# An mLSTM cell followed by a GELU block: the last weight conversion in the front's order, and two unread products

## The chip, the cores and the metric

The kernel runs on one core of a Trainium2 chip. The metric is the device time of one execution in microseconds. A core has a matrix engine (TensorE, PE in the profile; its weight loads are shown as PEld), a vector engine (VectorE, DVE), a scalar engine (ScalarE, ACT), a general engine (GpSimd, POOL) and a queue that issues the transfers (SyncE, SP). Each works through its own list of instructions and waits for the others by semaphores.

## The reference

Two blocks are computed one after the other. The first is a recurrent cell with 4 batches, 8 heads, 768 steps and head size 40, in float32:

```python
for t in range(S):
    m_new = np.maximum(f_gate[:, :, t] + m, i_gate[:, :, t])
    f_stab = np.exp(f_gate[:, :, t] + m - m_new)
    i_stab = np.exp(i_gate[:, :, t] - m_new)
    m = m_new
    C = f_stab[..., None, None] * C + i_stab[..., None, None] * np.einsum('bhd,bhe->bhde', vt, kt)
    n = f_stab[..., None] * n + i_stab[..., None] * kt
    h_tilde = np.einsum('bhde,bhe->bhd', C, qt)
    nq = np.einsum('bhd,bhd->bh', n, qt)[:, :, None]
    y[:, :, t] = sigmoid(o_gate) * h_tilde / np.maximum(np.abs(nq), 1.0)
```

The second takes y as x, of 3072 tokens by 320, and computes `gelu(x @ w_in) @ w_out` with w_in of 320 x 2048 and w_out of 2048 x 320. The weights arrive as float64 and are taken apart on the chip, as two 32-bit words each.

## The kernel before

The 768 steps are cut into 6 chunks ("cells") of 128, and each cell works on its 4 batches one after the other. Inside a cell the recurrence is written as matrix products: scores of keys and queries, weighed by decays, times the values, plus what the state of the cells before brings. The y of a cell (512 tokens) is transposed into x and goes through the up projection, GELU and down projection.

There is no scheduler: the order is written by hand. Each engine's list follows from the order in which the Python code emits the instructions. For the first stretch, "the front" (the first two cells, the conversion of all weights, and the first cell's up and down projection), the order is the string `FRONT`; each word is a letter for a step and, for most, a number of a batch. `play` runs it word by word. The words that matter here:

- `E`, `N`: `second_gates` and `later_gates`, the sums and running maxima of the gates of cell 1 and of cells 2 to 5 on VectorE, a store of the maxima, turns of `a` on TensorE (L216) and the two exponentials on ScalarE (L239, L240).
- `D`, `Q`: turns of the decays `ew` and `gg` into `ewT` and `gT` (TensorE L216, copies on VectorE L217). `d`, `q`: `decays_last`, a product with `last` (L249, tile `pd`) and its copy into `dec` (L251).
- `k2`: `warm(2)`, two products into a tile `cold` that nothing reads (L198). Each f32 product shows as two matmul records.
- `w`, `m`, `g`, `t`, `s`, `c`, `v`, `y`, `x`: steps of cell 0 for one batch (weights, mask, gate, turn, scores, carry, values, finish, turn of y); in capitals those of cell 1. `R`: `split_x`, which takes x_hi away from the transposed y (`px`) and writes x_lo and x_all on VectorE (L587, L588).
- `K`: `conv_one`, the first half of the conversion of the next piece of weights: VectorE L326, L331 and L333, with two ScalarE instructions, L328 and L329, between them. `J`: `conv_two`, the second half: VectorE L340 and L343. Pieces 0 to 9 are w_in, pieces 10 to 25 are the 16 rows of w_out. `J` also fetches the piece four further on, if there is one.
- `F`: one of the 16 rows of the first cell's down projection, four products with one row of w_out (L782, eight records). After the last row ScalarE copies the four results out (L787).
- `Z`: `split_weight`, which makes the high part of a w_in piece on ScalarE (L625) and its low part on VectorE (L627).

After the front, the loop over the cells calls `up` (L729 and L740: three products, of high, low and mixed parts, of each pair of w_in columns; the mixed weights are joined on VectorE, L633; GELU on ScalarE, L744) and then the down projection of the cell by seven products of sums (L805), between which the steps of the next cell are put by the string `DOWN`.

Tiles come from pools with a fixed number of buffers for a tag. Of weight here: `ps_tr` with two banks for all transposes (`pg`, `pd`, `pt`, `px`), `ps_h` with two banks for `cold`, `pf` and `ph`. A new tile waits until the one that had its buffer has been read.

Of the kernel before, what the change touches and what calls it, by code (L numbers as in the profile page):

```python
# [25 lines left out]


FRONT = """
    I2 O0 g0 L0 P0 L1 E k1 t0 P1 P2 k7 w0 N w1 O1 K L2 Q s0 O3 w2 q D d k2 P3 t1 w3 c0 L3 J v0 t2 K K y0 s1 I7 v1 I8
    O2 J g1 L4 I5 c1 K I1 I2 y1 s2 x0 t3 B4 O4 B5 g2 J x1 s3 v2 c2 L5 y2 H T0 x2 G0 v3 g3 c3 K y3 M1 J L6 J A x3 M0 K  # L30
    W0 O7 K A O6 O5 J M2 W1 S0 C0 K J J T1 U U K L7 V0 K T2 J J A G2 K G1 Y0 W2 S1 K M3 C1 A J S2 J K W3 K V1 C2 Y1
    T3 J J U U S3 V2 K K J G3 J Y2 C3 X0 K V3 J K F J F K K B8 F J K F F J K F F F R0 X1 J J K F J F K X2 F J K F J
    Y3 Z F R1 F K J B9 B10 F X3 R2 Z R3 F"""
DOWN = """
    M0 Z M1 W0 F L3 F W1 Z Z F S0 Z S1 K2 C0 M2 Z C1 G0 G1 G2 G3 V0 Z V1 W2 Z M3 F Q2 K3 Q3 Y0 D3 F F W3 F Z S2 S3
    C2 C3 V2 V3 F N F Y1 X0 R0 Y2 F F Y3 X1 R1 F X2 R2 F X3 R3 F"""
# [890 lines left out]
```

## Time and profile before

| what | us |
|---|---|
| three runs, middle one | 487.4 |
| the three runs | 485.79, 487.40, 490.38 |
| the profiled execution | 485.45 |
| its span, first to last instruction | 483.7 |
| TensorE busy | 474.4 |
| VectorE busy | 344.9 |
| ScalarE busy | 222.4 |
| granted TensorE clock, share of full | 1.00 |

The span is what the trace covers; the profiled execution's own time is 1.75 us longer. In the lines below, L followed by a number is a line of the kernel; `po<-w_out,g` is written from `w_out` and `g`; x with a number counts instructions; a bracket gives the time that the engine sat idle before the instruction and what ended that. Instructions on one engine overlap a little[...]. In the chain of waits the times are those of the chain alone, without overlap.

### The profile page before, as it was taken

The numbers are of one execution on the slowest core, as the hardware profiler recorded it, in microseconds if no ns is written. First come the engines' busy times: TensorE is split into PE (matmuls) and PEld (weight loads), VectorE is DVE, ScalarE is ACT, GpSimd is POOL, SyncE is SP. The second block draws the span as 40 slices with busy tenths as digits, with TensorE's granted clock in tenths as the row PEclk, the third lists the DMA queues.
The fourth block names the chain that finished last, engine by engine and source line by source line (L and its number), as shares of the span: only waits on it lengthen the run. The fifth ranks groups of instructions, "written<-read, shape, count | busy, mean of one in ns | idle before, by whom it ended". The sixth has DMA issues, their size and how long they took to land.

```text
span 483.7 us, 10808 instructions
## 1 busy us (share of the span) xinstructions
PE 474.4 (98%) x4224; PEld 415.5 (86%) x4224; DVE 344.9 (71%) x728; ACT 222.4 (46%) x477; POOL 70.2 (15%) x108
## 2 busy tenths in 40 slices
PE   8899999999999999999999999999999999999996
PEld 7687888877677999977999977999977899977996
DVE  7899699898979988747497857498757397724321
ACT  6977999844532942211961212961202861211300
POOL 3001210001000136200144200145000221000000
PEclk9999999999999999999999999999999999999999
DMA  9998965379320355931274922265921250100001
GB/s 176 200 216 185 191 160 138 102 174 224 95 26 4 40 113 75 209 59 21 31 145 67 200 41 25 30 134 94 184 42 22 32 87 3 54 3 0 1 1 54
DMA packets 164434, 44.24 MB, mean 91 GB/s; under 512 B 154176, under 2 KB 157408, under 8 KB 164384
## 3 DMA queue, kind: packets, MB, share of 16 engines
q1 hardware_dynamic: 164384, 43.56, 46.2%
q8 instruction: 33, 0.54, 0.5%
q14 instruction: 17, 0.14, 0.1%
HBM read 39.52 MB, written 4.01 MB: 90 GB/s over the span
## 4 chain that ended last, share of the span: by engine, by line
PE 79%; DVE 13%; ACT 3%; issue 1%; DMA 1%; POOL 1%; SPq 1%; DVEq 0%; POOLq 0%
PE po L805 30%; PE pu L729 21%; PE pu L740 6%; PE pu L674 5%; PE ps L471 5%; PE ph L534 4%; PE pf L495 2%; PE pf L490 2%; DVE w_out L343 1%; PE pu L680 1%; DVE pow L340 1%; PE px L569 1%; PE pt L445 1%; DVE W L474 1%; DMA W<-M_d 1%
## 5 line engine op out<-in xcount | busy, mean ns | idle before, releaser
L805 PE MATMUL po<-w_out,g 128*128 128x160 f32 x640 | 91.2, 300 | 0.0
L744 ACT ACTIVATE g<-pu 128x512 f32<-128x512 f32 x80 | 40.8, 614 | 108.2 <-PE pu L740 108.0
L805 PEld LDWEIGHTS po<-w_out,g 128*128 128x128 f32 x640 | 87.8, 190 | 1.8 <-ACT g L744 1.8
L402 ACT ACTIVATE W<-W,aT 128x128 f32<-128x128 f32 x160 | 48.9, 389 | 2.3 <-POOL W L376 2.2
L805 PE MATMUL po<-w_sums,sums 128*128 128x160 f32 x320 | 47.2, 302 | 0.0
L805 PEld LDWEIGHTS po<-w_sums,sums 128*128 128x128 f32 x320 | 44.2, 190 | 0.4
L579 ACT ACTIVATE x_hi<-px 128x384 fp32r<-128x384 f32 x20 | 9.8, 490 | 71.6 <-PE px L569 71.6
L729 PE MATMUL pu<-x_hi,w_in_hi 128*128 128x512 f32 x160 | 41.4, 401 | 0.0
L474 DVE TENSOR_TENSOR W<-ps,W 128x512 f32<-128x512 f32 x48 | 30.2, 683 | 15.2 <-ACT W L402 10.7
L729 PE MATMUL pu<-x_lo,w_in_lo 128*128 128x512 f32 x160 | 40.6, 396 | 0.0
L661 DVE TENSOR_TENSOR sums<-g 128x512 f32<-128x512 f32 x20 | 13.8, 690 | 33.3 <-ACT g L744 33.3
L376 POOL TENSOR_SCALAR_AFFINE_SELECT W<-W 128x1024 f32<-128x1024 f32 x20 | 23.1, 1162 | 92.7 <-DMA W<-M_d 92.4
L729 PEld LDWEIGHTS pu<-x_hi,w_in_hi 128*128 128x128 f32 x160 | 29.4, 188 | 8.2 <-ACT g L744 1.9
L782 PE MATMUL po<-w_out,g 128*128 128x320 f32 x128 | 35.3, 434 | 1.1 <-DVE w_out L343 1.1
L729 PEld LDWEIGHTS pu<-x_lo,w_in_lo 128*128 128x128 f32 x160 | 30.1, 188 | 7.2
L782 PEld LDWEIGHTS po<-w_out,g 128*128 128x128 f32 x128 | 24.0, 190 | 10.9 <-DVE w_out L343 1.4
L818 DVE TENSOR_TENSOR o_sb<-po,o_sb 128x320 f32<-128x320 f32 (+1 forms) x27 | 12.6, 465 | 28.3 <-PE po L805 24.4
L729 PE MATMUL pu<-x_all,w_in_mid 128*128 128x512 f32 x80 | 31.7, 396 | 0.1
L729 PE MATMUL pu<-x_all,w_mid 128*128 128x512 f32 x80 | 31.7, 396 | 0.0
L414 POOL MEMSET g<- 32x1024 f32 x8 | 7.6, 945 | 157.9 <-ACT W L402 157.7
L633 DVE TENSOR_TENSOR w_in_mid<-w_in_hi,w_in_lo 128x512 fp32r<-128x512 f32 x20 | 13.8, 688 | 21.6 <-PE pu L729 21.6
L674 PE MATMUL pu<-first_x,w_in 128*128 128x256 f32 x128 | 29.1, 382 | 0.1
(169 smaller groups left out, 884.2 us busy)
## 6 DMA issues: line engine op xcount, KB each, us to landing
W<-M_d SPq DMA_DIRECT2D x20, 512.0 KB, 5.7
bits<-in_moe_w_in_dram SPq DMA_DIRECT2D x20, 256.0 KB, 4.2
bits<-in_moe_w_out_dram SPq DMA_DIRECT2D x16, 320.0 KB, 3.5
ob<-in_o_gate_dram SPq DMA_DIRECT2D x24, 160.0 KB, 3.8
out_dram<-o_sb SPq DMA_DIRECT2D x24, 160.0 KB, 1.9
vb<-in_v_dram SPq DMA_DIRECT2D x22, 160.0 KB, 5.2
kb<-in_k_dram SPq DMA_DIRECT2D x22, 160.0 KB, 4.9
blocks<-in_k_dram SPq DMA_DIRECT2D x48, 32.0 KB, 2.2
```

Source lines behind the costliest of these rows:

```text
L376: nc.gpsimd.affine_select(out=t, in_=t, compare_op=OP.is_ge, fill=1.0e30, base=0, pattern=[[0, H], [1, L]], channel_multiplier=-1)
L402: nc.scalar.activation(out=W[n][:, h, :], in_=src, func=AF.Exp, scale=-1.0, bias=aT[:, self.c, r:r + 1])
L471: nc.tensor.matmul(ps[hip][:, p, :], kT[r, p, :], qT[r, p, :], start=True, stop=True)
L474: nc.vector.tensor_tensor(out=w, in0=ps[hip], in1=w, op=OP.mult)
L534: nc.tensor.matmul(ph[r, h, :], Pm[:, h, r], vb[turn_of(n)][:, h, :], start=True, stop=True)
L633: nc.vector.tensor_tensor(out=w_mid[i], in0=w_hi[i], in1=w_lo[i], op=OP.add)
L674: nc.tensor.matmul(banks[-1][e][:, i - i0, :], in_tile(i, x)[:, e, i % 2 * P:(i % 2 + 1) * P], first_x[:, x, t0:t1], start=(x == 0 and i = ...
L729: nc.tensor.matmul(pus[i][e], w[k][:, e, i * P:(i + 1) * P], x[:, k, :], start=(n == 0 and k == 0), stop=False, skip_group_check=True)
L740: nc.tensor.matmul(pu[e], w[r, i // 2, i % 2 * P:(i % 2 + 1) * P], x[r, NX, :], start=False, stop=(n == 2), skip_group_check=True)
L744: nc.scalar.activation(out=g.t[:, HF * e + i, :], in_=pu[e], func=AF.Gelu, scale=4097.0)
L782: nc.tensor.matmul(po[b], g.t[:, f, b * L:(b + 1) * L], w_out[:, f, :], start=(f == 0), stop=(f == NF - 1))
L805: nc.tensor.matmul(bank[at][:, i, :], lhs(j, t), rhs(j), start=(first and i == 0 and j == 0), stop=(i == n - 1 and j == HF - 1), skip_grou ...
```

## The change

Two places in the string `FRONT` are rewritten. Near its beginning one more `k2` is put behind `N`, and the `k2` that stood behind `d` is put ahead of it. At its end, the last `K` goes ahead of the row `F` that follows the finish of batch 3, the last `J` goes between the split of x1 and the next row, and the first `Z` goes behind that row. The list is printed anew, so line breaks in it move as well; words that are not named stay in their order.

```diff
-  ... k7 w0 N w1 O1 K L2 Q s0 O3 w2 q D d k2 P3 t1 ...
+  ... k7 w0 N k2 w1 O1 K L2 Q s0 O3 w2 q D k2 d P3 t1 ...
...
-  ... X2 F J K F J Y3 Z F R1 F K J B9 B10 F X3 R2 Z R3 F
+  ... X2 F J K F J Y3 K F R1 J F Z B9 B10 F X3 R2 Z R3 F
```

The instructions of TensorE are the same but for the two unread products (four records) that are new and the two that trade places with the product of `d`. On VectorE and ScalarE none is added; the conversion of piece 25 (`K`, `J`) comes ahead of the low and high weight of `Z`. The orders of GpSimd and SyncE are the same.

More of the change, by code (lines that the diff above doesn't have):

```diff
@@ L28 @@
 FRONT = """
[L29 to L33, printed above, removed]
+    I2 O0 g0 L0 P0 L1 E k1 t0 P1 P2 k7 w0 N k2 w1 O1 K L2 Q s0 O3 w2 q D k2 d P3 t1 w3 c0 L3 J v0 t2 K K y0 s1 I7 v1
+    I8 O2 J g1 L4 I5 c1 K I1 I2 y1 s2 x0 t3 B4 O4 B5 g2 J x1 s3 v2 c2 L5 y2 H T0 x2 G0 v3 g3 c3 K y3 M1 J L6 J A x3
+    M0 K W0 O7 K A O6 O5 J M2 W1 S0 C0 K J J T1 U U K L7 V0 K T2 J J A G2 K G1 Y0 W2 S1 K M3 C1 A J S2 J K W3 K V1 C2
+    Y1 T3 J J U U S3 V2 K K J G3 J Y2 C3 X0 K V3 J K F J F K K B8 F J K F F J K F F F R0 X1 J J K F J F K X2 F J K F
+    J Y3 K F R1 J F Z B9 B10 F X3 R2 Z R3 F"""
 DOWN = """
```

## The prediction

> **What bounds the kernel now.** I read the share of each engine first, then the chain of work that ended last, then who waited for whom at the two places that the diff touches, then the timeline there. The first view says that TensorE (PE) is the limit over the whole span, and the chain by engine says how much of the end is not TensorE's.
>
> ```profile
> PE 474.4 (98%) x4224; PEld 415.5 (86%) x4224; DVE 344.9 (71%) x728; ACT 222.4 (46%) x477; POOL 70.2 (15%) x108
> PE 79%; DVE 13%; ACT 3%; issue 1%; DMA 1%; POOL 1%; SPq 1%; DVEq 0%; POOLq 0%
> ```
>
> So only what makes TensorE wait, or what feeds the 13% of VectorE (DVE) on the chain, can count. The chain around the end of the front reads (start, us, work):
>
> ```profile
> 122.62 0.93 DVE y_rest L558
> 123.55 0.60 DVE w_in_lo L627
> 124.15 0.47 DVE x_lo L587
> 124.62 0.46 DVE x_all L588
> 125.08 0.24 DVE pow L326
> ...
> 125.35 0.57 ACT pow L328
> ...
> 127.07 0.50 DVE w_out L343
> 127.57 0.04 issue
> 127.62 2.42 PE po L782 x8
> 130.04 11.17 PE pu L729 x48
> ```
>
> The reader is to see that the eight products of the last row of the first down projection begin at 127.62, 0.05 us after VectorE has written the last w_out row. The wait in front of them is in the timeline of TensorE:
>
> ```profile
> 126.20 0.27 PE L569 MATMUL px<-ident,y_rest 128*128 128x128 f32 x1
> 127.62 2.42 PE L782 MATMUL po<-w_out,g 128*128 128x320 f32 x8 [1.14 <-DVE w_out L343]
> ```
>
> That idle time, 1.14 us, is all that TensorE has left at this place. The other place is the gates' turn near 19 us:
>
> ```profile
> 18.26 0.25 PE L216 MATMUL pg<-ident,gg 32*128 32x32 f32 x1
> 18.54 0.19 DVE L217 COPY gT<-pg 128x32 f32<-128x32 f32 x1 [0.17 <-PE pg L216]
> 18.79 0.41 PE L249 MATMUL pd<-gT,last 128*128 128x32 f32 x2 [0.28 <-DVE gT L217]
> 19.04 0.69 PE L198 MATMUL cold<-w_out 128*128 128x128 f32 x4
> 19.24 0.19 DVE L251 COPY dec<-pd 128x32 f32<-128x32 f32 x1 [0.50 <-PE pd L249]
> 19.56 0.60 PE L445 MATMUL pt<-ident,kb 128*128 128x128 f32 x4
> ```
>
> TensorE idles 0.28 us for gT, and VectorE 0.50 us for pd. One unread f32 product is two matmul records, so a k2 is the row "cold x4".
>
> **What the Trainium skill says.** "TensorE: Matmul & The Clock Gate", Part 1, says that TensorE runs at half clock until it has been busy for a window of about 3.4 us. The trace agrees: 12 cold matmuls took 2.75 us from 4.16 (0.23 each), 14 took 1.73 us from 9.22 (0.12 each), and later pt groups of four keep 0.60 us. So unread products have no clock to win at 12 to 20 us in this execution. "PSUM — Partial Sum Buffer", section "Engine vs sequencer instructions", says that VectorE's and ScalarE's queues are strictly first in, first out, and that matmuls complete in order. The records of this trace keep that order, so what is moved on VectorE moves everything behind it.
>
> **The change part by part.**
>
> *Conversion of piece 25 (w_out row 15).* Five VectorE and two ScalarE (ACT) instructions move; none is added or removed. SyncE's and GpSimd's orders are unchanged, and no load follows, for no piece is left to fetch. VectorE's order from the end of y_rest was: low weight, split of x1, first half of the conversion, second half, split of x2. It becomes first half, split of x1, second half, low weight, split of x2. The first slot stays where y_rest leaves it, at 123.47 (start of the low weight in the timeline). Durations from start to start: the first half followed by a split took 1.01 (L326 at 108.83, split at 109.84); a split took 0.94 (124.07 to the next work at 125.00 is 0.93); L340 took 0.52 (110.92 to 111.44) and L343 itself 0.49. So: split at 123.47 + 1.01 = 124.48; L340 at 125.42; L343 at 125.94, done at 126.43; products possible at 126.43 + 0.05 = 126.48. The two ScalarE steps lie beside the split: L328 began 0.35 after L326 and the pair ended 1.51 after it (125.00, 125.35, 126.51), so they end at 124.98, before 125.42. The former wait of 0.47 us for L329 is gone. TensorE is free at 126.20 + 0.27 = 126.47. The start moves from 127.62 to 126.48: **1.14 us less**; I take 1.1. Its ends: 0 if something else holds the products (below), 1.14 at most, since no idle time is left.
>
> What is late next? The low weight 0 starts at 126.34 in place of 123.47, split x2 at 126.94, low weight 1 at 127.87, split x3 at 128.47, ending at 129.40 (129.94 before, so 0.5 earlier). The low products started at 131.73 and would start at 130.6; x_lo is whole at 129.02. The mid products started at 133.60, now 132.5; their weights follow at 130.1 and 130.7. Cover remains in both, 1.6 and 1.8 us. On ScalarE the high weight 0 goes behind L329 and ends at 124.98 + 0.61 = 125.6, and VectorE wants it at 126.34. The transposes of x3 need the PSUM buffer that split x1 frees: 125.08 before, 125.49 now, against 125.98, when TensorE gets there; slack 0.49, cost nothing. The copies of po (ScalarE, four in 2.04 us) find high weight 1 done at 127.5, so they end near 129.5, ahead of the second pair of banks at 134.4.
>
> Does the gain travel? TensorE runs from 130.04 without a break in the chain to 142.14; then g on ScalarE, w_rest_hi, the low weights and sums on VectorE, and TensorE again at 154.10. Each link starts from the one before, so a whole chain shifts. VectorE idles 2.15 us before 141.06, waiting for buffers that these products free, so it has room.
>
> *k2 put ahead of d.* One product pair, 0.52 us (19.04 to 19.56), starts right after the turn of gg, at about 18.35 (18.26 and one spacing of such turns, (0.43 - 0.25) / 3 = 0.06 us, and rounding up). It ends issuing at 18.87, against 18.79, when gT is there. So pd and dec are 0.1 us late, at most 0.25 (if the pair starts at 18.51, after the turn's full record), and TensorE reaches pt 0.2 to 0.45 us sooner. Does being sooner help? VectorE works from dec at 19.24 to 31.44 with no idle time in its records, and TensorE meets it at the ph products at 26.82 (the W product of L474 ends at 26.87) and at px, 31.52, whose ob ends at 31.44. So TensorE would wait there, and VectorE's lateness travels: +0.1, between 0 and +0.25. Behind dec queue vw and the conversion of piece 0; pf at 21.41 needs vw, which ends at 19.84, so that wait is covered. Below nothing: the 0.18 us that VectorE waits at 31.62 could be saved, but px stays tied to ob, so I exclude more than 0.05.
>
> *New k2 behind N.* Four records of 0.13 us follow the turns of a (11.76, four of them, issuing done near 12.0), so they end near 12.52. The mask products pm were waiting for ScalarE's W until 12.62 (0.43 us idle). ScalarE takes that pm only after ew and gg, at 14.91. Cost nothing; if that cover were gone, 0.52. Nothing reads the tile; it takes one more turn of the pool of two.
>
> Sum: -1.1 + 0.1 + 0 = **-1.0 us**. The profiled execution took 485.45 us (span 483.7, 1.75 around it), so like it 484.45. The three runs shown are 485.79, 487.4 and 490.38; with the profiled one the middle of four is (485.79 + 487.4) / 2 = 486.6. Less 1.0 this is 485.6, which I predict; against the median of 487.4 it would be 486.4.
>
> **The rivals.** *The gain is taken back* (chance 0.2). TensorE starts earlier, but a later meeting with VectorE (the mid weights of pair 3, on the chain at 152.76) is set by VectorE's own 0.5 us instead of by TensorE's 1.1, or later than that by loads. For it: VectorE is busy 24.91 of the 29 us from 131 to 160. Against it: the 2.15 us hole. Time: 486.6 - 0.5 + 0.1 = 486.2, or 486.7 with nothing left.
>
> *Both places gain* (0.12). The idle 0.28 us before pd is filled for nothing and TensorE's lead of 0.44 us survives because VectorE catches up. Against it stands the unbroken work of VectorE. Time: 486.6 - 1.14 - 0.4 = 485.1.
>
> *Slower: unread products at the low clock* (0.13). The window's phase differs between executions. If TensorE is still at the rate of 4.16 us, a pair costs 4 x 0.23 = 0.92 us, two 1.84. Placed ahead of pd and pm, both would have to lie wholly on the chain; it decides from the point where they add more than 1.1 us. Then 486.6 + 1.84 - 1.1 = 487.3. For it: runs of one kernel spread over 4.6 us. Against it: pm has cover of over 2 us until 14.91.
>
> That the change does not do what it says is small here: the new order on VectorE and ScalarE is as the list of steps reads. My own case has 0.55.
>
> **How the numbers follow.** The range begins below the second rival on the profiled execution's level (485.45 - 1.54 = 483.9) and reaches over the slow rival on the level of the median (487.4 + 0.74 = 488.1): 483.8 to 488.4. A measurement of this kernel can tell about 1%, 4.9 us, from no change; every case lies far inside that. What remains is the scatter of the runs: faster 0.03, same 0.92, slower 0.05.
>
> **What would show it.** Right: the wait of the last L782 products for w_out under 0.2 us, they start about 1.1 us earlier counted from the first of them, the wait for L329 ahead of the last L340 gone, dec within 0.25 us of its place, and pu's first L729 group followed by the low products without a wait. Wrong: a wait of L569 for px's buffer, of L729 for x_lo or w_in_lo, a longer idle time before dec, or the start of the second cell's first po products (158.99 before) less than 0.6 us earlier.

## The result, and the profile after

Both kernels were run 22 times side by side: 484.19 us after (483.64 to 486.20) against 485.69 us before (484.14 to 490.38), both medians. The ratio is 0.9969, with a 95% interval of 0.9955 to 0.9983: 1.5 us (0.3%) less, and the whole interval lies below 1. The page of the changed kernel shows a span 1.2 us shorter, with four TensorE matmul records more (the new k2) and the same count on the other engines:

```profile
span 482.5 us, 10815 instructions
PE 474.3 (98%) x4228; PEld 415.3 (86%) x4228; DVE 348.3 (72%) x728; ACT 222.1 (46%) x477; POOL 69.8 (14%) x108
```

The chain of waits at the end of the front (start, us, work) now stays on TensorE:

```profile
115.58 10.77 PE po L782 x40
126.35 0.33 PE px L569 x3
126.68 0.04 issue
126.72 2.42 PE po L782 x8
129.14 11.15 PE pu L729 x48
```

In the chain of before, VectorE and ScalarE stood ahead of the last eight products; here the transposes of x3 do, by a narrow margin: w_out ended at 126.66. VectorE's own timeline shows the new order, and no wait for L329 in front of L340:

```profile
123.58 0.23 DVE L558 COPY y_rest<-ob 128x128 f32<-128x128 f32 x1
123.73 0.32 DVE L326 TENSOR_SCALAR pow<-bits 128x320 uint32<-128x320 uint32 x1
...
124.72 0.55 DVE L587 SCALAR_TENSOR_TENSOR x_lo<-px,x_hi 128x384 fp32r<-128x384 f32 x1
...
125.65 0.48 DVE L340 SCALAR_TENSOR_TENSOR pow<-bits,pow 128x320 uint32<-128x320 uint32 x1
126.17 0.49 DVE L343 SCALAR_TENSOR_TENSOR w_out<-sig,pow 128x320 f32<-128x320 f32 x1
126.58 0.69 DVE L627 SCALAR_TENSOR_TENSOR w_in_lo<-w_in_hi,w_in 128x512 fp32r<-128x512 f32 x1
```

At the gates' turn the two lines of VectorE are

```profile
18.61 0.19 DVE L217 COPY gT<-pg 128x32 f32<-128x32 f32 x1 [0.17 <-PE pg L216]
19.40 0.19 DVE L251 COPY dec<-pd 128x32 f32<-128x32 f32 x1 [0.59 <-PE pd L249]
```

From gT to dec it is 0.79 us; before it was 0.70 (18.54 to 19.24). TensorE's timeline has the `k2` ahead of pd:

```profile
18.51 0.71 PE L198 MATMUL cold<-w_out 128*128 128x128 f32 x4
19.05 0.31 PE L249 MATMUL pd<-gT,last 128*128 128x32 f32 x2
```

One execution differs from the next by some tenths of a microsecond before and between these places, so I compare distances inside a profile rather than times of day. "First to last row" is from the first L782 product to the first of the last eight; the mark of the stage after it is the first L805 product; "stage" is from there to the next up projection's first L729; "mask" is from the L805 mark to GpSimd's second mask of cell 2 (L376).

| distance, us | before | after | difference |
|---|---|---|---|
| gT copy to first L782 | 74.38 | 74.51 | +0.13 |
| first to last row of L782 | 34.70 | 33.60 | -1.10 |
| last row to first L805 | 31.30 | 31.28 | -0.02 |
| stage | 44.67 | 44.25 | -0.42 |
| mask | 20.87 | 20.39 | -0.48 |

So the profile's 1.2 us are the end's 1.1 and 0.42 us in a stage that the diff does not touch, less some tenths in which the front and the last cells took longer. That stage, and why the medians show 1.5, needed experiments.

The distance from the first to the last row has a scatter of its own: over all profiles of this study it is 34.68 to 35.01 in the six kernels with the old end and 33.39 to 33.73 in the six with the new one. A sharper measure starts at VectorE's "slot", the first instruction behind the last y_rest. Before, that is

```profile
123.47 0.68 DVE L627 SCALAR_TENSOR_TENSOR w_in_lo<-w_in_hi,w_in 128x512 fp32r<-128x512 f32 x1
```

and the products of the last row start at 127.62, 4.15 us later. After, it is L326 at 123.73, and the products start at 126.72, 2.99 us later. In all six kernels with the old end this path takes 4.14 or 4.15 us, in all six with the new end 2.99 or 3.00. What scatters is the place of the slot, 30.39 to 30.87 us behind the first row, and part of that is GpSimd's mask near 122 us (L376), which stretches one or another of the VectorE instructions ahead of it. In the changed profile it stretches L550 to 0.94 us (0.17 before), with the end and the new k2 it stretches L552 to 1.05 (0.49 before): 0.77 and 0.56 us lost, which is the 0.2 by which their slots differ (30.61 and 30.39).

### The profile page after: what moved, and what is told of

The parts are those of the page before. It is cut to its first block, busy times and chain, and to the rows that moved or that the text cites. A ratio compares the mean times of both kernels' runs of the same rounds, so it can differ in the third digit from the quotient of the medians.

```text
span 482.5 us, 10815 instructions
## 1 busy us (share of the span) xinstructions
PE 474.3 (98%) x4228; PEld 415.3 (86%) x4228; DVE 348.3 (72%) x728; ACT 222.1 (46%) x477; POOL 69.8 (14%) x108
## 4 chain that ended last, share of the span: by engine, by line
PE 89%; DVE 6%; DMA 1%; ACT 1%; issue 1%; SPq 1%; DVEq 0%
PE po L805 32%; PE pu L729 21%; PE po L782 7%; PE pu L740 6%; PE pu L674 5%; PE ps L471 4%; PE ph L534 4%; PE pf L495 3%; PE pf L490 2%; PE px L569 2%; PE pu L680 1%; DMA v<-in_v_dram 1%; ACT g L744 1%; PE pt L445 1%; SPq L135 1%
## 5 line engine op out<-in xcount | busy, mean ns | idle before, releaser
L805 PE MATMUL po<-w_out,g 128*128 128x160 f32 x640 | 91.2, 300 | 0.0
L805 PEld LDWEIGHTS po<-w_out,g 128*128 128x128 f32 x640 | 87.8, 190 | 1.8 <-ACT g L744 1.8
L805 PE MATMUL po<-w_sums,sums 128*128 128x160 f32 x320 | 47.2, 302 | 0.0
L805 PEld LDWEIGHTS po<-w_sums,sums 128*128 128x128 f32 x320 | 44.2, 190 | 0.4
L729 PE MATMUL pu<-x_hi,w_in_hi 128*128 128x512 f32 x160 | 41.4, 400 | 0.0
L729 PE MATMUL pu<-x_lo,w_in_lo 128*128 128x512 f32 x160 | 40.6, 396 | 0.0
L729 PEld LDWEIGHTS pu<-x_hi,w_in_hi 128*128 128x128 f32 x160 | 29.4, 188 | 8.2 <-ACT g L744 1.9
L729 PEld LDWEIGHTS pu<-x_lo,w_in_lo 128*128 128x128 f32 x160 | 30.1, 188 | 7.2
L376 POOL TENSOR_SCALAR_AFFINE_SELECT W<-W 128x1024 f32<-128x1024 f32 x20 | 22.5, 1132 | 91.4 <-DMA W<-M_d 74.5
L782 PE MATMUL po<-w_out,g 128*128 128x320 f32 x128 | 35.3, 434 | 0.0
L782 PEld LDWEIGHTS po<-w_out,g 128*128 128x128 f32 x128 | 24.0, 190 | 9.8 <-DVE w_out L343 0.3
L729 PE MATMUL pu<-x_all,w_in_mid 128*128 128x512 f32 x80 | 31.7, 396 | 0.1
L729 PE MATMUL pu<-x_all,w_mid 128*128 128x512 f32 x80 | 31.7, 396 | 0.0
```

The source lines that it names most:

```text
L376: nc.gpsimd.affine_select(out=t, in_=t, compare_op=OP.is_ge, fill=1.0e30, base=0, pattern=[[0, H], [1, L]], channel_multiplier=-1)
L729: nc.tensor.matmul(pus[i][e], w[k][:, e, i * P:(i + 1) * P], x[:, k, :], start=(n == 0 and k == 0), stop=False, skip_group_check=True)
L782: nc.tensor.matmul(po[b], g.t[:, f, b * L:(b + 1) * L], w_out[:, f, :], start=(f == 0), stop=(f == NF - 1))
L805: nc.tensor.matmul(bank[at][:, i, :], lhs(j, t), rhs(j), start=(first and i == 0 and j == 0), stop=(i == n - 1 and j == HF - 1), skip_grou ...
```

## The experiments

This is what the kernel before, the changed kernel and the twelve experiments gave. The last three columns sort the timed runs by their mean granted TensorE clock; "at full clock" is 0.998 or more. The kernel before was timed beside the experiments in four comparisons, which its row puts together; the median of its runs at full clock is 485.28 to 485.55 in the four, so a difference of 0.2 us between kernels of different comparisons says nothing. Its 22 runs beside the changed kernel have no clock on record and are not in the row.

| kernel | median us, runs | ratio to before, interval | runs at full clock, their median | 0.995 to 0.997 | under 0.995 |
|---|---|---|---|---|---|
| before | 486.31, 217 | | 118, 485.43 | 54 | 45 |
| changed | 484.19, 22 | 0.9969, 0.9955 to 0.9983 | 18, 484.11 | 4 | 0 |
| end only | 484.84, 22 | 0.9959, 0.9937 to 0.9980 | 13, 484.33 | 8 | 1 |
| both k2 only | 485.56, 22 | 0.9976, 0.9956 to 0.9996 | 19, 485.53 | 3 | 0 |
| Z behind only | 485.04, 22 | 0.9981, 0.9956 to 1.0006 | 13, 484.91 | 5 | 4 |
| K split only | 485.98, 22 | 0.9998, 0.9972 to 1.0024 | 10, 485.05 | 7 | 5 |
| eight ahead of d | 488.11, 12 | 1.0023, 0.9994 to 1.0052 | 5, 486.63 | 5 | 2 |
| eight behind N | 485.52, 20 | 0.9961, 0.9940 to 0.9981 | 20, 485.52 | 0 | 0 |
| W first | 489.13, 22 | 1.0049, 1.0025 to 1.0073 | 10, 487.87 | 9 | 3 |
| end, W first | 487.33, 22 | 1.0008, 0.9985 to 1.0032 | 13, 486.96 | 4 | 5 |
| end, new k2 | 484.67, 22 | 0.9972, 0.9952 to 0.9993 | 16, 484.47 | 5 | 1 |
| end, eight behind N | 483.95, 11 | 0.9958, 0.9941 to 0.9976 | 11, 483.95 | 0 | 0 |
| the same again | 484.37, 22 | 0.9962, 0.9947 to 0.9977 | 22, 484.37 | 0 | 0 |
| no k2 | 486.38, 22 | 1.0010, 0.9989 to 1.0031 | 10, 485.50 | 7 | 5 |

### The two halves of the change

End only:

```diff
-  ... Y3 Z F R1 F K J B9 B10 F X3 R2 Z R3 F
+  ... Y3 K F R1 J F Z B9 B10 F X3 R2 Z R3 F
```

> Only the end of the front is changed; the unread products stay as before. Theory A (the order of VectorE ahead of the last w_out row is all of the gain, the two k2 cost a little): the wait of the last L782 products falls from 1.14 to under 0.2 us, dec keeps its place at 19.24, the products of the first down projection begin at 92.9 as before, and the kernel is 1.1 to 1.6 us faster than before, as fast as the changed kernel or 0.1 us faster. Theory B (the unread products bring the gain, or half of it): less than 0.6 us faster.

Both k2 only:

```diff
-  ... k7 w0 N w1 ... q D d k2 P3 ...
+  ... k7 w0 N k2 w1 ... q D k2 d P3 ...
```

> Only the two k2 are changed; the end of the front stays as before. Theory A: pd about 0.1 us later counted from gT, VectorE behind it too, the first L782 product about 0.1 to 0.2 us later, the wait of 1.14 us for w_out unchanged, and the kernel 0 to 0.3 us slower, which the times can hardly tell from none. Theory B: 0.6 us faster or more.

With the end alone the distance from the first to the last row fell from 34.70 to 33.73, and TensorE's timeline shows what is left of the wait:

```profile
127.03 2.42 PE L782 MATMUL po<-w_out,g 128*128 128x320 f32 x8 [0.17 <-DVE w_out L343]
```

At full clock its runs are 485.43 - 484.33 = 1.1 us faster (1.0 against the 485.32 of the kernel before in the same comparison), the size forecast for the end. One expectation missed: the first row began at 93.30 and not near 92.9, 75.00 us behind gT in place of 74.38. With W first and the same front (below) it is 74.36, so this is one execution's scatter. With the two k2 alone the distance stayed at 34.69 and the wait at 1.13; gT to dec grew from 0.70 to 0.78 (18.55 to 19.33), gT to the first row by 0.06, and at full clock the runs are 0.1 us slower (0.2 in the same comparison). So theory A holds for both halves as far as runs at full clock go. Yet the ratio to before is 0.9976, with the whole interval below 1: the last columns of the table say why, and they come back below.

### The end, term by term

Z behind only:

```diff
-  ... Y3 Z F R1 F K J B9 B10 F X3 ...
+  ... Y3 F R1 F K J Z B9 B10 F X3 ...
```

> Of the end only one move: the first Z goes behind the last J; K and J stay together behind the split of x1. Theory A, term by term: the low weight's 0.60 us leaves the path to w_out row 15, the wait for L329 (0.47 us) stays, so the wait of the last L782 products is 1.14 - 0.60 = 0.54 us and the kernel about 0.6 us faster. Rival (the wait of the last products is set by something beside VectorE's list): the wait stays near 1.14 or goes at once.

K split only:

```diff
-  ... Y3 Z F R1 F K J B9 B10 F X3 ...
+  ... Y3 Z K F R1 J F B9 B10 F X3 ...
```

> Of the end only the other move: the conversion's first half ahead of the split of x1 and its second half behind it, with the first Z still ahead of both. Theory A, term by term: VectorE has 0.60 of low weight, 1.01, 0.94, 0.52 and 0.49 us to do from 123.47, so w_out is there at 127.03 and the wait is about 0.6 us; the wait for L329 is gone; the kernel is about 0.5 us faster. With the run in which only Z goes behind, the two gains add up to the whole 1.1. Rival: as there.

The slot on VectorE and the last row on TensorE with only Z behind:

```profile
123.52 0.55 DVE L587 SCALAR_TENSOR_TENSOR x_lo<-px,x_hi 128x384 fp32r<-128x384 f32 x1
127.06 2.42 PE L782 MATMUL po<-w_out,g 128*128 128x320 f32 x8 [0.62 <-DVE w_out L343]
```

and with only K split, where the transposes of x3 (px) are of interest too:

```profile
123.62 0.68 DVE L627 SCALAR_TENSOR_TENSOR w_in_lo<-w_in_hi,w_in 128x512 fp32r<-128x512 f32 x1
126.38 0.41 PE L569 MATMUL px<-ident,ob 128*128 128x128 f32 x2
126.63 0.27 PE L569 MATMUL px<-ident,y_rest 128*128 128x128 f32 x1
127.22 2.42 PE L782 MATMUL po<-w_out,g 128*128 128x320 f32 x8 [0.32 <-DVE w_out L343]
```

From the first to the last row they measure 34.18 and 34.19: 0.52 and 0.51 us gained, where 0.60 and about 0.5 were forecast (the waits forecast were 0.54 and 0.6). Counted from the slot the scatter is gone: 127.06 - 123.52 = 3.54 and 127.22 - 123.62 = 3.60, so 0.61 and 0.55 less than before, together the 1.16 of the whole (4.15 - 2.99). With K split the bracket says 0.32, not 0.6. The rest of the wait has moved ahead of px: from the first row to px it is 126.38 - 93.03 = 33.35 us, and 125.98 - 92.92 = 33.06 before. The split of x1 now ends at 126.24 (125.69 and 0.55, from VectorE's timeline), and px, which starts 0.14 us later, needs the buffer that it frees. This is the slack of 0.49 us in the prediction, overrun by 0.29; in the full change the split ends early enough and px keeps its place (126.19 - 93.12 = 33.07).

The gain at full clock is 0.5 us for Z and 0.4 for K (0.4 and 0.3 in the same comparison). Over all their runs neither interval lies wholly below 1, so the profiles show these two gains and the times alone do not. The profile of the K run nevertheless has the span of before, 483.7: its stage took 45.07 us. That is the second thing to explain.

### The stage that the diff does not touch

Ordering the profiles by the time of the mask (those with another order on SyncE's queue come below) gives the answer without another kernel (distances as above, us):

| profile | mask | stage |
|---|---|---|
| no k2 | 20.15 | 44.25 |
| end, new k2 | 20.19 | 44.25 |
| eight behind N | 20.22 | 44.25 |
| changed | 20.39 | 44.25 |
| end, eight behind N, again | 20.48 | 44.26 |
| eight ahead of d | 20.56 | 44.35 |
| end only | 20.57 | 44.35 |
| both k2 only | 20.72 | 44.52 |
| Z behind only | 20.77 | 44.56 |
| before | 20.87 | 44.67 |
| end, eight behind N | 20.88 | 44.67 |
| K split only | 21.28 | 45.07 |

In this table the stage is 44.25 us up to a mask at 20.47; past that each tenth of the mask is a tenth of the stage (K split: 21.28 - 20.47 + 44.25 = 45.06). The mask waits for the transfer of W. GpSimd's timeline before has it so:

```profile
179.79 1.09 POOL L376 TENSOR_SCALAR_AFFINE_SELECT W<-W 128x1024 f32<-128x1024 f32 x1 [7.62 <-DMA W<-M_d]
```

and after:

```profile
178.39 1.09 POOL L376 TENSOR_SCALAR_AFFINE_SELECT W<-W 128x1024 f32<-128x1024 f32 x1 [7.13 <-DMA W<-M_d]
```

The load of W stands on SyncE's queue behind 16 block loads, whose pace varies from one execution to the next: W was issued 15.5 to 16.8 us after the mark. Kernels with the old end and kernels with the new one are found at both ends of the table (no k2 and before; end with new k2 and end with eight), so nothing shows the 0.42 us by which the two first profiles differ here to be a property of the change. To see whether the order on that queue could be mended:

```diff
-            load_blocks(self.c * B + b, self.by_block)
+            load_blocks(self.c * B + b, self.by_block, (0,))
+
+        def load_last_q(self, b):
+            load_blocks(self.c * B + b, self.by_block, (1,))
...
-  ... G3 V0 Z V1 ...
+  ... G3 V0 B3 Z V1 ...
```

Here the argument chooses k (0) or q (1) in `load_blocks`, and B in `DOWN` is the new step.

> The kernel before, with one change far from the diff: of the 16 block loads for the fourth batch the eight of q are issued behind the values of batch 0, so the loads of W<-M_d for the next masks stand ahead of them on SyncE's queue. Theory C (the stage from 158 to 203 is as long as these W loads make it, through SyncE's queue of loads; seen so far: W issued 15.91 to 16.83 us after the first L805 product, and the stage to the next up projection 44.25 to 45.07 us, in the same order): W is issued about 12 to 13 us after it, the mask of 179.79 comes up to 3 us sooner, the ph products of 184.69 wait for nothing, and the stage is 44.2 to 44.3 us, as in the changed kernel; the whole kernel is 0.2 to 0.8 us faster. Rival (the stage's length has another cause, or the q blocks, now later, hold the scores of batch 3): 44.6 us or more.

> The end of the front changed, the unread products as before, and W ahead of the q blocks as in the run on the kernel before. Theories A and C together: the wait for w_out row 15 under 0.2 us and the stage from the first L805 product to the next up projection 44.2 to 44.3 us; 1.5 to 1.9 us faster than before, and the fastest kernel of the study. Rival: no faster than with the end alone, 1.1 us faster than before.

Both miss in the stage and in the time, though with the end changed the wait for w_out is 0.17 us, as expected. W was issued 11.95 us after the mark and the mask came at 175.27, 4.5 us sooner, as theory C has it; but the rival was right about what comes next. The chain of waits of the kernel with W first (its lines are numbered two or five higher: L162 loads W and L147 the blocks, L160 and L145 before; L427 turns q and L476 are the scores, L422 and L471 before):

```profile
170.91 0.34 SPq L162
...
172.41 3.02 SPq L147
...
178.66 2.24 DMA g<-in_q_dram
...
181.02 0.71 DVE qT L427
...
182.53 1.16 PE ps L476 x14
```

The q blocks are now last, VectorE waits 3.3 us for them with everything behind it, and the scores of batch 3 wait for VectorE. The stage is 45.25 us (158.96 to 204.21), and the later cells lose as well (73.44 us to the next up projection, 72.96 before); the kernel is 0.5% slower, and at full clock 2.4 us. With the end's change it is 2.6 us slower than the end alone (486.96 and 484.33, from two comparisons). The queue's order was the better of the two.

### The two k2 in larger doses

Eight ahead of d, on the kernel before:

```diff
-  ... q D d k2 P3 ...
+  ... q D k8 d P3 ...
```

> The kernel before, with the unread products behind d put ahead of it and made eight (k8): the moved k2 in a larger dose. Theory A (VectorE works without a gap from dec on, so what pd is late travels to the end of the front): eight products are 16 records of 0.13 us, 2.1 us from 18.51, so pd starts near 20.6 in place of 18.79 and dec near 20.9 in place of 19.24; the first L782 product begins 1.5 to 1.8 us later than 92.92 and the kernel is 1.5 to 1.8 us slower. Rival (later idle time of VectorE and TensorE takes it up): under 0.6 us later at the first L782 product.

Eight behind N, on the kernel before:

```diff
-  ... k7 w0 N w1 ...
+  ... k7 w0 N k8 w1 ...
```

> The kernel before, with eight unread products (k8) behind N: the new k2 in a larger dose. Theory A (its place is covered, since ScalarE takes the mask product behind it only at 14.91 and the turns of ew and gg wait for ScalarE till 14.34 and 15.05): the 16 records end near 14.2 in place of nothing, the two mask products follow, the turn of gg is at most 0.3 us late, and the first L782 product and the kernel move by 0 to 0.3 us. Rival (no cover): 1.5 us or more.

TensorE's timeline with the eight ahead of d, then VectorE's dec:

```profile
17.94 2.05 PE L198 MATMUL cold<-w_out 128*128 128x128 f32 x16
19.83 0.31 PE L249 MATMUL pd<-gT,last 128*128 128x32 f32 x2
```

```profile
20.17 0.19 DVE L251 COPY dec<-pd 128x32 f32<-128x32 f32 x1 [1.93 <-PE pd L249]
```

From gT (18.05) to dec it is 2.12 us in place of 0.70: 1.42 late. From gT to the first row it is 93.83 - 18.05 = 75.78 in place of 74.38: 1.40 late. What dec is late goes through to the end of the front whole, as forecast, and at full clock the kernel is 1.2 us slower (five runs; 1.1 in the same comparison); the rival of under 0.6 falls. The forecast of 1.5 to 1.8 was too high because the sixteen records take 1.89 us up to pd (0.118 each) and not 2.1.

Behind N they cost nothing:

```profile
11.83 2.05 PE L198 MATMUL cold<-w_out 128*128 128x128 f32 x16
13.72 0.39 PE L397 MATMUL pm<-M_parts,row 96*128 96x128 bf16 x4
```

The mask products now start at 13.72 and 14.16, ScalarE takes them from 14.41, and from gT (18.33) to the first row it is 74.37 us, as before. Its last row lies 35.01 us behind the first, the longest of all; the path from the slot is 4.15 us, as before, so this is the slot's scatter. At full clock the kernel is as fast as before (485.52, and 485.55 in the same comparison). The same kernel had 20 runs of 20 within 0.9 us.

### What the unread products behind N do

By then 33 of 142 runs of the kernel before had a granted clock below 0.995 and took some 490 us. That made a fourth theory, D.

End and new k2, the other k2 left behind d:

```diff
-  ... k7 w0 N w1 ...
+  ... k7 w0 N k2 w1 ...
-  ... Y3 Z F R1 F K J B9 B10 F X3 R2 Z R3 F
+  ... Y3 K F R1 J F Z B9 B10 F X3 R2 Z R3 F
```

> The end of the front changed and the new k2 behind N, but the other k2 left behind d, as before. Theory D (the scatter of the runs comes from the TensorE clock in the front, and the unread products behind N hold it: in the runs so far a granted clock under 0.995 and some 490 us were seen in 33 of 142 runs of the kernel before and in none of 64 with products behind N): no run under a clock of 0.995, none 3.5 us above the fastest. Theory A: the first L782 product begins 0.1 us earlier than with the k2 moved (F15 wait under 0.2 us), the median 484.0 to 484.3, as the changed kernel or 0.1 us below it. Rival to D (the k2 ahead of d holds the clock): some 5 of 22 runs near 489.

The same with k8 in place of the new k2:

> The end of the front changed and eight unread products behind N, the other k2 behind d. Theory D: with the larger dose no run under a clock of 0.998, as in the run of the eight on the kernel before (20 of 20 within 0.9 us); median 484.1 to 484.5, the span of all runs under 1.5 us. Rival: some 4 of 22 runs 1.5 us above, as in the changed kernel.

> The same kernel as the end with eight products behind N, run again, since it had only 11 runs and is the candidate for the fastest. Theory D: again no run under a clock of 0.998; median 483.8 to 484.3, ratio to the kernel before about 0.996. Rival (the 11 runs were luck): 2 of 11 or more at least 1.2 us above the fastest.

No k2:

```diff
-  ... q D d k2 P3 ...
+  ... q D d P3 ...
```

> The kernel before without the k2 behind d, so with no unread product between the first mask products and the scores of batch 0's successor. Theory D: as many runs near 490 as in the kernel before or more (5 of 22 or more, clock under 0.995), the other runs as before, 485.0 to 485.7, since TensorE reaches pt 0.5 us sooner but VectorE does not. Rival (the scatter has nothing to do with unread products): the same count as in the run with products behind N, 0 or 1 of 22.

With eight behind N no run of 53 (20 + 11 + 22) was below a clock of 0.998. With two there (changed, both k2 only, end and new k2) 1 of 66 was below 0.995 and 12 more below 0.998. With none there, 45 of 217 and 54 more in the kernel before, and 25 of 144 and 45 more in the other seven kernels. The rival that the k2 ahead of d does it falls with the eight ahead of d (2 of 12, and 5 more) and with the end and new k2, where none stands ahead of d. So D holds in its main point, by dose. Without any k2 there were 5 of 22, and the others were at 485.50, both as D expects. Some numbers were off. The end with the new k2 had one long run (488.23), a median of 484.67 in place of 484.3 at most, and its first row did not come sooner than in the changed kernel, though dec did (gT to dec 0.69, gT to first row 93.16 - 18.52 = 74.64). The end with eight had a median of 483.95, below the range given. Repeated, it kept its clock in all 22 runs, but four of them lay 1.2 us or more above the fastest (the longest 486.46), which is just the count that the rival named: its scatter is small, though not all of a run's scatter is the clock.

The counts differ between comparisons too: the kernel before had 15 of 75, 18 of 67, 8 of 48 and 4 of 27 runs below 0.995; of the 22 runs of the kernel before beside the changed one, only one was near 490, and the end alone, with nothing behind N, had one in 22. In which stretch of an execution the clock is lost was not seen, since no profile caught such an execution. That the few tenths of idle time between 12 and 15 us are where it begins is argued from where the products work, not shown.

The end with eight behind N beats the kernel before by 0.9958 and 0.9962 (each interval below 0.998). Its medians, 483.95 and 484.37, lie on both sides of the changed kernel's 484.19, so it is not shown to be faster than that, only to have no run at a lower clock.

## Why the prediction was right, and where it was not

*The time.* The forecast was 485.6 us, and the changed kernel took 484.19. Of these 1.4 us, 0.9 lie in the level: the middle of four runs was taken as 486.6, and 22 runs of the kernel before have a median of 485.69. The other 0.5 are the difference, -1.0 forecast and -1.5 measured. The range of 4.6 us held every case considered, no gain among them, so that 484.19 lies in it says little; what can be judged are the terms. The 1% that a measurement was said to tell apart was too coarse: the interval here is 0.28% wide.

*The end, -1.14, taken as -1.1.* Right, by mechanism and by size: 1.10 us in the profile, 1.1 at full clock with the end alone. The list of VectorE from the slot was worked out as 126.48 - 123.47 = 3.01 us and measures 2.99; the parts add up as worked out, 0.60 for the low weight and 0.55 for the split of the conversion. One bound was too tight. The 1.14 us of idle time was counted from the end of the px record, and no more was said to be left. The next products start sooner behind px than that: where w_out was in time (end and new k2), the distance from px to them was 0.33 us (126.22 to 126.55) against 1.64 before, so TensorE stood 1.31 us. That the two figures of 1.14, one from TensorE's records and one from VectorE's list, agreed was chance. The changed profile keeps 0.2 of the 1.31 as a wait; with the earlier slot of the end and new k2 nothing is left of it.

*What is late next.* Right: neither the low nor the mid products waited. Low weight 0 started at 126.58, the low products at 130.80, the mid products at 132.68. The buffer of px was the nearest danger, as said, and the K split shows it biting.

*k2 ahead of d, +0.1.* Right in size: dec 0.09 late from gT, and 0.1 or 0.2 us at full clock with both k2. But two steps were off and nearly cancel. The pair started 0.18 us behind the turn of gg (18.33 to 18.51) and not 0.09, so pd started 0.44 us behind gT in place of 0.25, 0.19 late, inside the 0.25 named as the most. Its two records then took 0.31 us in place of 0.41; why is not shown. At the first row a delay of 0.1 is below the scatter (74.51 us behind gT in the changed profile, but also with only K split, whose front is that of before). The dose of eight shows that VectorE carries it on: 1.42 late at dec, 1.40 at the first row.

*New k2 behind N, nothing.* Right for the profiled execution and wrong for the kernel. The eight cost nothing there, so the cover is as described. But the step "unread products have no clock to win at 12 to 20 us in this execution" was used for all executions. In others there is clock to win, and the prediction left that out: it took the spread of 485.79 to 490.38 for plain scatter. The rival built on the window's phase saw that executions differ, but with the wrong sign: products were to cost more at a low clock, and in the runs they make a low clock rarer. With the two k2 alone the timed runs are 0.24% faster, though 0.1 or 0.2 us slower at full clock.

*The sum, -1.0.* At full clock 485.43 - 484.11 = 1.3 us, in the medians of the paired runs 1.5. The full-clock figures come from different comparisons, so 0.2 or 0.3 of that I cannot assign; nor can it all be the clock, since the paired runs of before held one long run only.

*The rivals.* "The gain is taken back" did not happen as drawn (mid weights of pair 3), though a later stage with a transfer did take back 0.4 us in the K split's profile, and is as much shorter in the changed one. "Both places gain" is out as drawn, since the k2 moves gain nothing at full clock; what they gain comes with the clock. "Slower" is out.

## What to carry to other kernels

A wait behind a list that runs strictly in order is shortened by moving what does not feed it behind what does, and the gain can be added up from start-to-start times; then look for what the moved work held, here a transpose's buffer with half a microsecond of slack. A profile is one execution: before a difference of a few tenths in an untouched stage is given to a change, line up several profiles by the event that the stage waits for. And look at the granted clock of every run, not of the profiled one: here unread products in a place where the profile showed neither cost nor gain did away with a lower clock in one run of five.

## What the runs showed of the hardware that was not expected

- A mean granted clock of about 0.99 over the whole execution went with some 4.6 us more (490.07 against 485.43 for the kernel before), 0.995 to 0.997 with 1.3 us more (486.77); with 16 unread records in 2.05 us near 12 us neither was seen in 53 runs. "TensorE: Matmul & The Clock Gate", Part 1, in the Trainium skill speaks of windows of about 3.4 us whose phase is free. The rate at the start does differ between executions: the same twelve unread records took 2.75 us at 4.16 in the profile before and 2.26 us at 4.19 in the one after. The idle stretches between 12 and 15 us are under 0.5 us each, but every profile is of an execution at 0.999 or 1.00, so whether these windows account for the others stays open.
- SyncE's issues can stand for microseconds among many loads, and longer with a large one ahead: with W first (512 KB, issued at 170.91) one q block stood for 3.02 us, until 175.43; in the same stretch of the kernel before the longest stand of a block was 1.69. W landed at 175.12, but with the end changed too a block stood 3.33 us, until 0.93 after W had landed, so what it waits for is not shown.
- GpSimd's mask of about 1.1 us stretches the VectorE instruction that it meets. The mask at 122 us met y_rest before (0.93 us in place of 0.23) and L550 after (0.94 in place of 0.17). "SBUF — State Buffer", section "Who interferes with whom", in the Trainium skill says that VectorE shares a pair of ports with GpSimd, and that a VectorE instruction with two inputs in SBUF contends with a GpSimd instruction that reads SBUF. VectorE's timeline of the kernel with only K split agrees, where the mask (121.94 to 123.03) met a product of two such inputs that takes 0.49 before, and which ended 0.35 behind the mask:

```profile
122.13 1.25 DVE L552 TENSOR_TENSOR ob<-ob,den 128x320 f32<-128x320 f32 x1
```
